# One GpSimd addition rewritten with a column, and another written-out order of the program, in a clustered attention and MoE kernel

## The chip, the cores and the metric

The kernel runs on one core of a Trainium2 chip. The metric is the time of one execution on the device in microseconds (us). The core has five instruction streams that run side by side, each in its own order: PE (TensorE matmuls, with PEld for the loading of weights), DVE (VectorE), ACT (ScalarE), POOL (GpSimd) and SP (the queue that issues DMA transfers). An instruction starts when those ahead of it on its own engine are done and when the semaphores that it waits for are set.

## The reference

```python
q_assign = argmax(q_n @ c_n)            # nearest of 16 centroids, per head
k_assign = argmax(k_n @ c_n)
mask = q_assign[:, :, :, None] == k_assign[:, :, None, :]
scores = where(mask, scale * q @ k.T, -1e9)
attn = softmax(scores);  x = attn @ v   # 4 batches, 8 heads, 768 tokens, 64 columns a head
# x as 3072 tokens x 512
h = x @ w_in                            # 512 -> 2048
P = a[0] + a[1] * h + a[2] * h**2 + a[3] * h**3
Q = 1.0 + abs(b[0]) * abs(h) + abs(b[1]) * h**2
out = (P / (Q + 1e-6)) @ w_out          # 2048 -> 512
```

The change stands where `Q + 1e-6` is formed.

## The kernel before

**The work.** A batch `b` has four pairs of heads `hp`. `prep` loads and scales one pair's q and k, splits them into two float16 parts and finds the clusters; `attend` (batches 1 to 3) and `attend_keys` (batch 0) compute the scores and the attention for the pair, in three blocks of tokens `tb` of 256 tokens. In `attend` every tile of 128 queries x 768 keys goes PE (L987) to DVE (L1016, scaling and minimum) to ACT (the exponential) to DVE (L1035, reciprocal) to ACT and DVE (L1047, the two float16 parts) to a DMA transpose to PE (L1067). The weights of both layers are split into float16 parts while batch 0 is attended; this is the first 200 us or so.

**The gate.** `moe(b, tb)` runs the two layers for 256 tokens. It takes the 2048 hidden columns in 8 pieces: `ci` from 0 to 3 and `h` 0 or 1, each a tile of 128 x 512 float32. There are 12 blocks, so 96 pieces. For one piece: PE makes `ph` (L1274); ACT makes `u` (the absolute value, scaled) and `t`; DVE adds the polynomial's terms to `t` (L1291, L1292); then POOL squares, `s = (u + BT) * u` (L1336, L1337); ACT makes `u = exp(-ln(s + cq))`, the reciprocal of the denominator, where `cq` is a column that holds 1 + 1e-6; POOL adds that same constant to `s` in place (**L1354**, only where ACT has not done it before, in 44 of the pieces) and multiplies `s` by `u` (L1359), a step of refinement; `t = (t + a0) * u` is done on POOL (L1365, L1366) or on DVE (L1372); DVE makes the gate's value, `t = (s - 2) * t` (L1377); ACT copies its high float16 part (L1381), POOL forms the low one (L1385), and PE multiplies both with `w_out` (L1396) into `po`. In the last batch DVE does the work of L1359 (as L1348), of L1366 (as L1372) and of L1385.

**The order.** Every operation of the program is first recorded by `op`, in the order of the code, and then emitted in the order of a table of 4,187 numbers, `ORDER`. What stands on one engine is thus that engine's part of the table. The numbers such as 2150 in `op("POOL", 2150, ...)` are costs for the program that searched the order; nothing reads them when the kernel is built:

```python
    def op(self, eng, ns, fn, r=(), w=(), vt=0.0, claim=(), co=(), chain=None, n=None):
        self.ops.append(fn)
...
        for i in ORDER:
            self.ops[i]()
```

Tiles come from rings of a few buffers (`s`, `u`, `t` from a ring of 12), so an operation that takes a new buffer also waits until the old contents are done with.

Of the kernel before, what the change touches and what calls it, by code (L numbers as in the profile page):

```python
# [61 lines left out]
3 376 377 28 374 4 5 375 6 7 40 8 9 379 381 10 29 382 383 32 30 388 31 391 380 34 392 44 384 41 385 489 386 42  # L62
490 387 398 43 389 46 390 394 35 395 38 393 399 36 492 37 11 70 39 494 47 396 487 50 495 48 488 33 496 501 49
400 504 45 88 505 71 51 74 72 511 397 401 402 73 403 92 76 404 493 405 89 497 407 90 91 406 408 77 498 93 409
499 80 82 52 500 78 502 79 503 81 12 507 602 506 53 508 54 55 56 57 410 512 509 412 411 510 414 83 413 416 67
415 86 418 68 13 84 420 419 64 14 58 417 603 422 59 378 421 424 491 65 423 426 75 85 15 428 513 60 427 16 605
18 429 61 600 514 430 62 601 425 607 432 63 431 17 433 66 118 19 515 434 516 112 87 606 610 608 435 611 609
517 94 518 113 20 614 520 119 617 120 69 521 114 122 612 121 116 519 436 613 95 615 522 438 115 437 124 21 96
439 440 123 130 616 22 618 442 620 453 441 621 715 23 454 455 716 443 624 523 622 456 625 525 524 713 125 527
526 24 529 25 97 528 531 98 131 619 533 26 623 126 444 99 127 106 103 530 128 104 532 718 154 117 534 714 720  # L70
27 132 535 445 109 721 537 536 134 110 539 446 538 457 111 447 722 458 541 107 540 448 100 129 543 542 449 719
545 450 108 727 459 451 544 626 460 105 133 730 546 461 160 135 155 158 627 547 101 102 452 164 628 548 470
462 156 629 463 723 472 471 724 157 725 474 473 630 172 159 476 475 726 631 136 161 632 477 162 549 635 137
# [12 lines left out]
279 293 696 688 299 294 270 698 774 697 2 300 700 689 295 272 296 702 701 275 673 334 302 297 301 1267 674 699
690 322 675 303 703 775 676 1268 1263 677 691 776 276 304 692 335 693 678 694 336 273 777 338 305 337 1395 306
704 695 307 328 308 339 778 309 717 364 323 365 326 324 319 325 1396 320 1397 779 1251 705 1398 329 366 327
1269 340 706 330 332 780 331 367 781 316 707 792 1222 333 313 794 1270 782 708 1271 317 793 1399 1272 796 341
1401 1400 709 798 342 310 314 783 1404 343 1402 344 710 368 311 1223 1403 1224 1273 345 1274 795 1226 369 1407  # L90
1275 370 346 784 797 315 1278 1225 809 347 1276 1405 799 348 1228 811 312 349 1277 785 800 350 1227 1535 351
1408 321 355 2215 711 1536 352 356 1409 358 786 371 810 1229 787 359 372 813 801 353 1230 788 802 815 789 812
373 803 1231 1411 814 1282 1232 1410 361 1233 1283 1290 1533 816 804 1534 1406 1234 2216 817 2217 1291 712
1235 1284 354 1236 1237 790 1292 360 1285 805 1286 357 1293 1287 1294 806 1412 818 1288 807 791 819 1279 1238
820 1289 1538 1413 1394 821 1295 1414 2219 318 1540 822 1298 1541 1539 823 1542 1415 826 1544 1280 1299 362
1547 827 1296 1281 1300 1306 824 1301 2218 842 1302 363 1239 1548 828 843 1240 1303 1307 1678 829 1679 825
1304 844 2221 831 1308 830 1318 845 1319 858 2220 847 1309 832 3208 1310 859 846 1311 1297 834 1305 833 1312
874 848 808 860 1543 836 835 1313 1326 849 861 1416 875 863 1327 1320 862 1241 1328 852 1321 876 1322 890 837
1323 877 891 1324 1545 838 878 864 1334 850 1329 3209 839 1330 1417 1314 865 3210 2222 1335 851 841 1331 3212
1315 1418 853 866 1325 1336 879 840 1546 1332 854 868 1337 1333 1316 1342 892 1421 855 1317 1550 1338 1537  # L100
1343 906 1339 867 1551 1344 907 1419 880 869 856 1345 893 895 1346 1340 870 857 1347 894 1341 881 871 1354 896
2223 1348 2224 908 882 872 897 1355 1349 1422 884 1676 2225 1362 1552 909 1420 922 1363 1356 1677 883 910 898
923 1357 3211 911 1358 873 885 1364 1359 1350 900 1365 886 1366 1351 1360 1367 924 1370 1368 887 912 1371 925
1378 899 1352 888 1553 3213 1353 1379 1554 1423 1372 889 1361 926 914 1369 1242 1565 938 927 1373 901 913 1380
939 1374 916 902 915 958 1549 1381 1375 1382 1383 1376 903 959 940 1384 1377 928 1424 905 941 917 1681 1425
942 943 1680 1433 960 1385 918 1426 1555 3214 961 930 1434 929 1427 904 919 1556 1243 944 932 921 1428 1435
1429 962 1430 920 1557 1436 963 945 1437 1431 1438 946 1441 1432 1439 931 1683 964 1442 1449 1682 1386 947
1450 1443 1387 1684 1451 948 966 974 1440 1558 1388 1444 1452 1389 965 1453 1445 933 975 1244 1446 949 1454
990 967 976 1447 934 991 1559 977 1448 979 1455 950 1461 3215 978 1456 1469 992 935 1470 980 993 951 936 1462
1471 968 1560 1006 1463 994 981 1007 1472 1464 1562 982 3216 1465 1473 969 1466 1457 995 1563 1474 1467 1458  # L110
1008 1245 1468 1477 970 984 1475 1459 952 1009 1460 996 1476 1478 1485 1708 971 937 1486 1479 983 1010 1685
1487 953 1480 1566 1488 997 1481 1022 1489 985 1482 998 1687 1490 1023 1011 1483 954 1491 1484 956 1497 1024
2226 1000 957 972 999 986 1492 1025 1498 1505 987 1012 1686 973 1001 1499 1688 1506 2227 1690 988 1014 1026
1500 1002 1038 1507 1561 1501 1689 1691 1003 1693 1564 1039 1502 1694 1027 2242 989 1508 1013 1040 1509 1503
1493 1510 1043 1028 1504 1513 1511 2240 1004 1029 1514 2243 1041 1015 1494 1692 1515 1042 1521 1016 1495 1516
1030 1005 1696 1522 1044 1512 1054 1045 1517 1697 1567 1017 1518 1496 1055 1523 1032 1031 2244 1018 1070 1519
2228 1524 1056 1019 1525 1033 1520 1568 1526 1071 1046 1569 1034 1057 1059 1527 1020 1570 1058 1528 1072 1576
955 1035 1571 1060 1021 1572 2241 1577 1573 1709 1037 1073 1574 1047 1061 1074 1578 1698 1575 1048 1579 1062
1580 1584 2229 1581 1699 1036 1585 2245 1075 1700 1529 1586 1582 1530 1587 1049 1063 1076 1592 1583 1531 1588
1695 1589 1090 1532 1701 1593 1077 1050 1078 2247 1091 1080 1594 1051 2248 2246 1590 2249 1064 1595 1092 2251  # L120
1591 1604 2250 1702 1093 1106 1596 1605 2272 1079 1703 1052 1597 1065 1095 1606 1107 1598 1066 1607 2254 1608
# [1364 lines left out]
```

## Time and profile before

| | |
|---|---|
| median of 3 runs | 996.66 us (996.2 to 999.1) |
| the profiled execution's own time | 999.17 us |
| its span, from the first to the last instruction | 997.4 us |
| granted share of the TensorE clock | 0.979 |
| busy: PE, DVE, ACT, POOL | 881.2, 861.6, 803.7, 812.0 us |

The profile shows one execution. An engine's busy time is what its instructions took, waiting for the port or the semaphore inside an instruction included. In the rows below, `<-` in a name reads "out<-in"; after a gap it names what the engine waited for.

### The profile page before, as it was taken

The numbers are of one execution on the slowest core, as the hardware profiler recorded it, in microseconds if no ns is written. First come the engines' busy times: TensorE is split into PE (matmuls) and PEld (weight loads), VectorE is DVE, ScalarE is ACT, GpSimd is POOL, SyncE is SP. The second block draws the span as 40 slices with busy tenths as digits, with TensorE's granted clock in tenths as the row PEclk, the third lists the DMA queues.
The fourth block names the chain that finished last, engine by engine and source line by source line (L and its number), as shares of the span: only waits on it lengthen the run. The fifth ranks groups of instructions, "written<-read, shape, count | busy, mean of one in ns | idle before, by whom it ended". The sixth has DMA issues, their size and how long they took to land.

```text
span 997.4 us, 20735 instructions
## 1 busy us (share of the span) xinstructions
PE 881.2 (88%) x7705; PEld 583.8 (59%) x7705; DVE 861.6 (86%) x1522; ACT 803.7 (81%) x1524; POOL 812.0 (81%) x801
## 2 busy tenths in 40 slices
PE   1689998988898989989889989999899898999997
PEld 1357666765465546556556656665476564676663
DVE  6878998687898989989888999899899988788886
ACT  5468778998897889888888889898798887877574
POOL 4548778999999999999999999999989999343342
PEclk9979998999999999999999999999999999999999
DMA  7985576787857678767778868777876665411000
GB/s 222 232 218 128 170 176 180 189 184 147 154 97 149 117 156 150 149 122 148 145 145 157 128 135 162 153 138 103 162 130 130 115 127 101 81 43 38 1 33 21
DMA packets 358933, 132.99 MB, mean 133 GB/s; under 512 B 335280, under 2 KB 351664, under 8 KB 358832
## 3 DMA queue, kind: packets, MB, share of 16 engines
q1 hardware_dynamic: 358832, 131.67, 64.5%
q8 instruction: 60, 0.98, 0.4%
q14 instruction: 41, 0.34, 0.1%
HBM read 41.98 MB, written 6.29 MB: 48 GB/s over the span
## 4 chain that ended last, share of the span: by engine, by line
POOL 44%; PE 23%; DVE 14%; ACT 8%; issue 7%; DMA 4%; SPq 0%; ACTq 0%; POOLq 0%; DVEq 0%
POOL s L1354 7%; POOL s L1337 7%; POOL s L1359 6%; PE po L1396 6%; PE ph L1274 6%; POOL s L1385 6%; POOL s L1336 4%; POOL t L1366 4%; POOL t L1365 3%; DMA rwi<-in_moe_w_in_dram 2%; PE px L1174 2%; DVE s L1016 2%; DVE ah L1047 2%; PE s L1111 1%; PE s L987 1%
## 5 line engine op out<-in xcount | busy, mean ns | idle before, releaser
L1274 PE MATMUL ph<-x,win 128*128 128x256 f16 x2304 | 272.5, 274 | 8.9 <-DVE t L1292 5.3
L1396 PE MATMUL po<-wout,s 128*128 128x512 f16 x1008 | 249.8, 387 | 27.0 <-POOL s L1385 25.9
L1274 PEld LDWEIGHTS <-win 128*128 128x128 f16 x2304 | 224.9, 98 | 57.0 <-DVE t L1292 6.8
L1396 PEld LDWEIGHTS <-s 128*128 128x128 f16 x1008 | 95.8, 99 | 137.6 <-POOL s L1385 39.3
L1016 DVE TENSOR_SCALAR_CACHE_REDUCE s<-s,cc 128x768 f32<-128x768 f32 x144 | 145.7, 1016 | 15.9 <-PE s L987 15.6
L1047 DVE SCALAR_TENSOR_TENSOR ah<-s,su,ah 128x768 f16<-128x768 f32 x144 | 144.6, 1009 | 6.4 <-ACT ah L390 5.8
L390 ACT ACTIVATE ah<-s,su 128x768 f16<-128x768 f32 x144 | 128.0, 897 | 20.1 <-DVE su L1035 19.2
L987 PE MATMUL s<-sk,sq 128*128 128x384 f16 x576 | 118.8, 330 | 22.9 <-DVE ah L1047 21.8
L390 ACT ACTIVATE s<-s,nm 128x768 f32<-128x768 f32 x144 | 125.6, 872 | 15.7 <-DVE s L1016 13.7
L1377 DVE SCALAR_TENSOR_TENSOR t<-s,t 128x512 f32<-128x512 f32 x84 | 93.7, 1118 | 28.6 <-POOL s L1359 21.7
L1337 POOL TENSOR_TENSOR s<-s,u 128x512 f32<-128x512 f32 x84 | 111.2, 1324 | 7.0
L1359 POOL TENSOR_TENSOR s<-s,u 128x512 f32<-128x512 f32 x72 | 96.0, 1336 | 1.3 <-ACT u L390 0.2
L1336 POOL TENSOR_SCALAR s<-u,g 128x512 f32<-128x512 f32 x84 | 70.1, 835 | 30.9 <-ACT u L390 27.4
L987 PEld LDWEIGHTS <-sq 128*128 128x128 f16 x576 | 51.1, 98 | 73.4 <-DVE ah L1047 33.5
L1354 POOL TENSOR_SCALAR s<-s 128x512 f32<-128x512 f32 x44 | 88.7, 2016 | 4.6 <-ACT u L390 0.7
L1385 POOL TENSOR_TENSOR s<-t,s 128x512 f16<-128x512 f32 x72 | 89.3, 1241 | 2.8 <-ACT s L1381 1.5
L1067 PE MATMUL px<-at,vhi 128*64 128x256 f16 x864 | 75.7, 277 | 3.6 <-DVE t L1292 2.8
L390 ACT ACTIVATE u<-ph,gk 128x512 f32<-128x512 f32 x84 | 57.5, 684 | 15.4 <-PE ph L1274 14.7
L1381 ACT CAST s<-t 128x512 f16<-128x512 f32 x84 | 51.8, 616 | 18.4 <-DVE t L1377 18.3
L390 ACT ACTIVATE t<-ph,gk 128x512 f32<-128x512 f32 x84 | 65.2, 776 | 1.7 <-POOL s L1385 1.7
L1291 DVE SCALAR_TENSOR_TENSOR t<-ph,gk,t 128x512 f32<-128x512 f32 x84 | 62.2, 740 | 4.3 <-ACT t L390 4.2
L1292 DVE SCALAR_TENSOR_TENSOR t<-t,gk,ph 128x512 f32<-128x512 f32 x84 | 62.8, 748 | 3.0
(225 smaller groups left out, 1810.1 us busy)
## 6 DMA issues: line engine op xcount, KB each, us to landing
rwi<-in_moe_w_in_dram SPq DMA_DIRECT2D x16, 512.0 KB, 4.3
rwo<-in_moe_w_out_dram SPq DMA_DIRECT2D x16, 512.0 KB, 4.1
rk<-in_k_dram SPq DMA_DIRECT2D x32, 192.0 KB, 3.2
rq<-in_q_dram SPq DMA_DIRECT2D x32, 192.0 KB, 3.5
rvm<-in_v_dram SPq DMA_DIRECT2D x16, 384.0 KB, 3.9
rv<-in_v_dram SPq DMA_DIRECT2D x16, 384.0 KB, 3.9
out_dram<-ob SPq DMA_DIRECT2D x24, 256.0 KB, 2.7
at<-ah SPq DMA_TRANSPOSE x144, 4.0
```

The costliest lines, as they stand in the source:

```text
L390: lambda: nc.scalar.activation(out=out(), in_=in_(), func=func, **{a: (x() if callable(x) else x) for a, x in kw.items()}),
L987: nc.tensor.matmul(sc.ap[:, i, :SH], lhsT=st["q" + x].ap[:, j, t, :], rhs=st["k" + x].ap[:, j, ks, :].rearrange("p t c -> p (t c)"), start ...
L1016: lambda nm=nm, view=view: ts(out=view(), in0=view(), scalar1=cc.ap[:, 0:1], scalar2=None, op0=ALU.mult, op1=ALU.min, accum_out=nm.ap),
L1047: lambda part=part, view=view, su=su: stt(out=part(1), in0=view(), scalar=su.ap, in1=part(0), op0=ALU.mult, op1=ALU.subtract),
L1274: nc.tensor.matmul(ph.ap[:, fi * TW : (fi + 1) * TW], lhsT=win[:, wpart, c, f * P : (f + 1) * P], rhs=xs[c].ap[:, xpart], start=(i == 0), ...
L1336: nc.gpsimd.tensor_scalar(out=sv(), in0=uv(), scalar1=g1c(BT), scalar2=1.0, op0=ALU.add, op1=ALU.mult)
L1337: nc.gpsimd.tensor_tensor(out=sv(), in0=sv(), in1=uv(), op=ALU.mult)
L1354: lambda sv=sv: nc.gpsimd.tensor_scalar(out=sv(), in0=sv(), scalar1=1.0, scalar2=1e-6, op0=ALU.add, op1=ALU.add),
L1359: lambda uv=uv, sv=sv: nc.gpsimd.tensor_tensor(out=sv(), in0=sv(), in1=uv(), op=ALU.mult),
L1377: lambda tv=tv, sv=sv: stt(out=tv(), in0=sv(), scalar=2.0, in1=tv(), op0=ALU.subtract, op1=ALU.mult),
L1385: lambda tv=tv, g16=g16, e=(nc.vector if kshare("gld", b, i_) else nc.gpsimd): e.tensor_tensor(out=g16(1), in0=tv(), in1=g16(0), op=ALU.su ...
L1396: nc.tensor.matmul(po[ti].ap, lhsT=g16(gg)[:, c0 : c0 + P], rhs=wout[:, wpart, f, :], start=(i == 0 and f == 0), stop=(i == 2 and f == NF ...
```

## The change

In L1354 the two immediate additions become one addition of the column `cq`, which the kernel already holds, and a multiplication by one. The table `ORDER` is replaced by another one. The costs handed to the search change in eleven places, of which three stand here.

```diff
 ORDER = [int(i) for i in """
-3 376 377 28 374 4 5 375 6 7 40 8 9 379 381 10 29 382 383 32 30 388 31 391 380 34 392 44 384 41 385 489 386 42
+3 376 377 28 374 4 5 375 6 7 40 8 9 379 381 10 29 382 383 32 30 388 31 391 380 34 392 44 384 41 385 489 393
...
-                    op("POOL", (2150, 3450)[k], square, [*us, g1], ss, uu + kb("sq", b), [s_t, u_t])
+                    op("POOL", (2260, 3450)[k], square, [*us, g1], ss, uu + kb("sq", b), [s_t, u_t])
...
                     if not acq: op(
                         "POOL", (820, 1250)[k],
-                        lambda sv=sv: nc.gpsimd.tensor_scalar(out=sv(), in0=sv(), scalar1=1.0, scalar2=1e-6, op0=ALU.add, op1=ALU.add),
+                        lambda sv=sv: nc.gpsimd.tensor_scalar(out=sv(), in0=sv(), scalar1=cq, scalar2=1.0, op0=ALU.add, op1=ALU.mult),
                         [], ss, uu + kb("e", b) - 0.5, [s_t],
                     )
...
-                        (750, 1280)[k] if last else (1158, 2000)[k],
+                        (880, 1280)[k] if last else (1050, 2000)[k],
...
-                    (690, 1220)[k] if last else (972, 1700)[k],
+                    (840, 1220)[k] if last else (1100, 1700)[k],
```

The new table is a reshuffle over short distances: on each engine nearly all instructions stand within ten places of where they stood. Two places in batch 1's first block show its kind. In the names, `s1_0_1_0` is the tile `s` of batch 1, block 0, piece `ci` 1, `h` 0; the last number is a running one and differs between the two programs.

POOL before, at the second and third gate pieces of that block:

```order
L1354 TENSOR_SCALAR s1_0_0_1_5813<-s1_0_0_1_5813 128x512
L1385 TENSOR_TENSOR s0_2_3_1_5545<-t0_2_3_1_5543,s0_2_3_1_5545 128x512
L1365 TENSOR_SCALAR t1_0_0_0_5742<-t1_0_0_0_5742,gk1_2791 128x512
L1366 TENSOR_TENSOR t1_0_0_0_5742<-t1_0_0_0_5742,u1_0_0_0_5717 128x512
L1359 TENSOR_TENSOR s1_0_0_1_5813<-s1_0_0_1_5813,u1_0_0_1_5755 128x512
L1336 TENSOR_SCALAR s1_0_1_0_5954<-u1_0_1_0_5905,g11_2793 128x512
L1337 TENSOR_TENSOR s1_0_1_0_5954<-s1_0_1_0_5954,u1_0_1_0_5905 128x512
L1385 TENSOR_TENSOR s1_0_0_0_5738<-t1_0_0_0_5742,s1_0_0_0_5738 128x512
L1354 TENSOR_SCALAR s1_0_1_0_5954<-s1_0_1_0_5954 128x512
```

And POOL of the changed kernel at the same pieces:

```order
L1365 TENSOR_SCALAR t1_0_0_0_5743<-t1_0_0_0_5743,gk1_2792 128x512
L1366 TENSOR_TENSOR t1_0_0_0_5743<-t1_0_0_0_5743,u1_0_0_0_5719 128x512
L1385 TENSOR_TENSOR s0_2_3_1_5636<-t0_2_3_1_5552,s0_2_3_1_5636 128x512
L1354 TENSOR_SCALAR s1_0_0_1_5834<-s1_0_0_1_5834,cq_76 128x512
L1336 TENSOR_SCALAR s1_0_1_0_5934<-u1_0_1_0_5870,g11_2794 128x512
L1337 TENSOR_TENSOR s1_0_1_0_5934<-s1_0_1_0_5934,u1_0_1_0_5870 128x512
L1359 TENSOR_TENSOR s1_0_0_1_5834<-s1_0_0_1_5834,u1_0_0_1_5813 128x512
L1354 TENSOR_SCALAR s1_0_1_0_5934<-s1_0_1_0_5934,cq_76 128x512
L1385 TENSOR_TENSOR s1_0_0_0_5740<-t1_0_0_0_5743,s1_0_0_0_5740 128x512
```

The product for `t1_0_0_0` (L1365, L1366) moved ahead of the addition L1354 of the next piece.

DVE before, where that product is used (L1377 of `t1_0_0_0`):

```order
L1016 TENSOR_SCALAR s1_3_5_1_5829,nm1_3_5_1_5879<-s1_3_5_1_5829,cc1_3_4194 128x2x384
L1372 SCALAR_TENSOR_TENSOR t1_0_0_1_5836<-t1_0_0_1_5836,gk1_2791,u1_0_0_1_5755 128x512
L1047 SCALAR_TENSOR_TENSOR ah1_3_5_0_5900<-s1_3_5_0_5821,su1_3_5_0_5859,ah1_3_5_0_5900 128x768
L1035 RECIPROCAL su1_3_5_1_5913<-su1_3_5_1_5913 128x1
L1377 SCALAR_TENSOR_TENSOR t1_0_0_0_5742<-s1_0_0_0_5738,t1_0_0_0_5742 128x512
L1083 SCALAR_TENSOR_TENSOR x1_3_1_5948<-px1_3_1_5881,x1_3_1_5948 128x256
L1377 SCALAR_TENSOR_TENSOR t1_0_0_1_5836<-s1_0_0_1_5813,t1_0_0_1_5836 128x512
```

And DVE of the changed kernel there:

```order
L1016 TENSOR_SCALAR s1_3_5_1_5843,nm1_3_5_1_5872<-s1_3_5_1_5843,cc1_3_4285 128x2x384
L1377 SCALAR_TENSOR_TENSOR t1_0_0_0_5743<-s1_0_0_0_5740,t1_0_0_0_5743 128x512
L1035 RECIPROCAL su1_3_5_0_5864<-su1_3_5_0_5864 128x1
L1035 RECIPROCAL su1_3_5_1_5896<-su1_3_5_1_5896 128x1
L863 COPY tk22_1_5930<-tk12_1_5315 128x12x64
L1372 SCALAR_TENSOR_TENSOR t1_0_0_1_5839<-t1_0_0_1_5839,gk1_2792,u1_0_0_1_5813 128x512
L1047 SCALAR_TENSOR_TENSOR ah1_3_5_0_5938<-s1_3_5_0_5820,su1_3_5_0_5864,ah1_3_5_0_5938 128x768
```

L1377 of `t1_0_0_0` moved ahead of L1372 and L1047.

## Rows read from the trace of the kernel before

**Rows 1.** The page, part 1 (busy time, share of the span, instructions) and part 4 (the chain that ended last: its shares by engine, then by line).
```profile
PE 881.2 (88%) x7705; PEld 583.8 (59%) x7705; DVE 861.6 (86%) x1522; ACT 803.7 (81%) x1524; POOL 812.0 (81%) x801
POOL 44%; PE 23%; DVE 14%; ACT 8%; issue 7%; DMA 4%; SPq 0%; ACTq 0%; POOLq 0%; DVEq 0%
POOL s L1354 7%; POOL s L1337 7%; POOL s L1359 6%; PE po L1396 6%; PE ph L1274 6%; POOL s L1385 6%; POOL s L1336 4%; POOL t L1366 4%; POOL t L1365 3%; DMA rwi<-in_moe_w_in_dram 2%; PE px L1174 2%; DVE s L1016 2%; DVE ah L1047 2%; PE s L1111 1%; PE s L987 1%
```

**Rows 2.** Busy time by stretch: the stretch in us, its length, busy us and instructions of PE, PEld, DVE, ACT, POOL, then the granted clock, the DMA share and GB/s.
```profile
0.00:100.00 100.00, 65.06 (x661) 45.14 (x662) 79.09 (x172) 62.51 (x112) 57.47 (x78) 0.95 0.80 200
100.00:200.00 100.00, 91.03 (x1104) 65.91 (x1103) 84.53 (x164) 81.40 (x157) 82.64 (x100) 0.97 0.70 179
200.00:300.00 100.00, 87.32 (x787) 59.22 (x784) 82.69 (x158) 89.25 (x181) 95.72 (x93) 0.97 0.74 144
600.00:700.00 100.00, 93.37 (x810) 61.80 (x806) 93.75 (x174) 88.61 (x175) 93.97 (x91) 1.00 0.76 140
900.00:950.00 50.00, 49.83 (x369) 33.98 (x368) 42.13 (x60) 33.96 (x55) 18.19 (x17) 1.00 0.07 20
200.00:850.00 650.00, 583.61 (x4934) 379.87 (x4931) 577.83 (x1019) 561.10 (x1094) 616.50 (x577) 0.98 0.73 139
```

**Rows 3.** The same view in slices of 25 us, the two with the busiest PE and the busiest DVE.
```profile
600.00:625.00 25.00, 22.56 (x221) 15.33 (x217) 24.89 (x42) 23.36 (x48) 22.82 (x19) 1.00 0.83 159
725.00:750.00 25.00, 24.79 (x220) 17.75 (x218) 22.41 (x42) 24.11 (x47) 22.06 (x20) 1.00 0.78 147
```

**Rows 4.** Groups of POOL's instructions from 200 to 850 us: busy us, mean ns of one, then idle time ahead of them.
```profile
L1354 POOL TENSOR_SCALAR s<-s 128x512 f32<-128x512 f32 x44 | 88.7, 2016 | 4.6 <-ACT u L390 0.7 <-ACT su L390 0.4
L1336 POOL TENSOR_SCALAR s<-u,g 128x512 f32<-128x512 f32 x72 | 59.0, 819 | 4.0 <-ACT su L390 2.1 <-ACT u L390 0.4
L1365 POOL TENSOR_SCALAR t<-t,gk 128x512 f32<-128x512 f32 x43 | 35.0, 813 | 0.5
```

**Rows 5.** Single lines: duration ns min/median/max, then first and last start in us.
```profile
L1354 POOL TENSOR_SCALAR s<-s x44: 1922/1928/2532, 217.1 to 836.3; 128x512 f32<-128x512 f32 x44
L1336 POOL TENSOR_SCALAR s<-u,g x84: 685/695/1650, 212.9 to 971.3; 128x512 f32<-128x512 f32 x84
L1365 POOL TENSOR_SCALAR t<-t,gk x43: 687/696/1401, 223.0 to 839.6; 128x512 f32<-128x512 f32 x43
L1377 DVE SCALAR_TENSOR_TENSOR t<-s,t x84: 666/1024/2117, 222.2 to 982.8; 128x512 f32<-128x512 f32 x84
L1372 DVE SCALAR_TENSOR_TENSOR t<-t,gk,u x41: 727/868/1754, 218.4 to 979.2; 128x512 f32<-128x512 f32 x41
```

**Rows 6.** Timeline of POOL, start us and duration us, at the pieces whose order is shown above and a little later.
```profile
431.36 1.92 POOL L1354 TENSOR_SCALAR s<-s 128x512 f32<-128x512 f32 x1
433.36 1.16 POOL L1385 TENSOR_TENSOR s<-t,s 128x512 f16<-128x512 f32 x1
434.49 1.13 POOL L1365 TENSOR_SCALAR t<-t,gk 128x512 f32<-128x512 f32 x1
435.71 1.26 POOL L1366 TENSOR_TENSOR t<-t,u 128x512 f32<-128x512 f32 x1
...
450.11 0.69 POOL L1365 TENSOR_SCALAR t<-t,gk 128x512 f32<-128x512 f32 x1
450.89 1.27 POOL L1366 TENSOR_TENSOR t<-t,u 128x512 f32<-128x512 f32 x1
```

**Rows 7.** Timeline of DVE at the same pieces, the idle time ahead and its releaser in brackets.
```profile
433.43 1.63 DVE L1372 SCALAR_TENSOR_TENSOR t<-t,gk,u 128x512 f32<-128x512 f32 x1
437.01 1.74 DVE L1377 SCALAR_TENSOR_TENSOR t<-s,t 128x512 f32<-128x512 f32 x1 [0.94 <-POOL t L1366]
```

**Rows 8.** The chain that ended last, in the stretch from 200 to 850 us, by line.
```profile
by line: POOL s L1354 10.5%; POOL s L1337 10.1%; POOL s L1359 9.9%; POOL s L1385 9.6%; issue 7.7%; POOL s L1336 6.2%; POOL t L1366 6.1%; POOL t L1365 3.9%; PE po L1396 3.1%; DVE s L1016 2.8%; DVE ah L1047 2.7%; POOL vlo L963 2.1%; PE ph L12
```

**Rows 9.** Waits from 200 to 850 us: who waited for whom, us in total, times, longest.
```profile
PE po L1396 <- POOL s L1385: 25.9, 23, 2.9
PE s L987 <- DVE ah L1047: 21.8, 29, 2.4
DVE t L1377 <- POOL s L1359: 21.7, 15, 4.0
DVE s L1016 <- PE s L987: 12.3, 17, 3.0
```

**Rows 10.** Groups of DVE's instructions that read two tiles of SBUF, from 200 to 850 us, and L1377 again from 500 to 600 us (the third row).
```profile
L1377 DVE SCALAR_TENSOR_TENSOR t<-s,t 128x512 f32<-128x512 f32 x72 | 83.0, 1155 | 28.4 <-POOL s L1359 21.7 <-POOL t L1366 6.6
L1372 DVE SCALAR_TENSOR_TENSOR t<-t,gk,u 128x512 f32<-128x512 f32 x29 | 29.9, 1030 | 0.0
L1377 DVE SCALAR_TENSOR_TENSOR t<-s,t 128x512 f32<-128x512 f32 x11 | 14.6, 1330 | 4.6 <-POOL s L1359 4.0 <-POOL t L1366 0.6
```

**Rows 11.** Timeline around one L1354, POOL and DVE.
```profile
670.06 1.95 POOL L1354 TENSOR_SCALAR s<-s 128x512 f32<-128x512 f32 x1
...
671.05 0.67 DVE L1377 SCALAR_TENSOR_TENSOR t<-s,t 128x512 f32<-128x512 f32 x1
...
671.72 0.73 DVE L1372 SCALAR_TENSOR_TENSOR t<-t,gk,u 128x512 f32<-128x512 f32 x1
...
672.09 1.38 POOL L1385 TENSOR_TENSOR s<-t,s 128x512 f16<-128x512 f32 x1
```

More of the change, by code (lines that the diff above doesn't have):

```diff
@@ L739, in g_scale @@
         dve(160, bound2, [], [g1], vt)
-        op("POOL", 1090, square_term, [aab], [g1], vt)
+        op("POOL", 1300, square_term, [aab], [g1], vt)
         act(250, lambda: g1c(R1), lambda: g1c(X1), AF.Ln, [], [g1], vt)
         act(250, lambda: g1c(R1), lambda: g1c(R1), AF.Exp, [], [g1], vt, scale=0.5)
-        dve(690, root, [], [g1], vt, n=4)
+        dve(950, root, [], [g1], vt, n=4)
         op("POOL", 1460, bound3, [aab], [g1], vt)
@@ L836, in prep @@
         dve(471, k_scale, [pb], [ks], u)
-        op("POOL", 1250, q_scale2, [ks], [qs, cc], u)
+        op("POOL", 1450, q_scale2, [ks], [qs, cc], u)
         dve(157, lambda: nc.vector.reciprocal(out=qs.ap[:, 1:2], in_=qs.ap[:, 0:1]), [], [qs], u)
@@ L855, in prep @@
                 dve(
-                    1500,
+                    1340,
                     lambda nm=nm, sc=sc, hi=hi, lo=lo: stt(
@@ L862, in prep @@
                 )
-            dve(575, lambda nm=nm, hi=hi: nc.vector.tensor_copy(out=cols(nm + "2", 0), in_=cols(nm + "1", hi)), [one], [two], u)
+            dve(730, lambda nm=nm, hi=hi: nc.vector.tensor_copy(out=cols(nm + "2", 0), in_=cols(nm + "1", hi)), [one], [two], u)
         def turn(x, u):
@@ L881, in fixed_rows @@
                 nc.gpsimd.memset(rows("q2"), 0.0)
-            op("POOL", 700, fixed_rows, [], [tm["k2"], tm["q2"]], vt + kb("p2", b, 2))
+            op("POOL", 1100, fixed_rows, [], [tm["k2"], tm["q2"]], vt + kb("p2", b, 2))
         for x in ("k1", "q1"):
@@ L1009, in attend @@
                     act(
-                        1170, view, view, AF.Exp, [nm, cc], [sc, su], u + kb("exp", b),
+                        1085, view, view, AF.Exp, [nm, cc], [sc, su], u + kb("exp", b),
                         bias=lambda nm=nm: nm.ap, scale=lambda: cc.ap[:, 1:2], accum_out=lambda su=su: su.ap,
@@ L1014, in attend @@
                     dve(
-                        1156,
+                        1076,
                         lambda nm=nm, view=view: ts(
@@ L1021, in attend @@
                     act(
-                        1071, view, view, AF.Exp, [nm], [sc, su], u + kb("exp", b),
+                        992, view, view, AF.Exp, [nm], [sc, su], u + kb("exp", b),
                         bias=lambda nm=nm: nm.ap, scale=-1.0, accum_out=lambda su=su: su.ap,
@@ L1346, in moe @@
                     dve(
-                        (770, 1300)[k] if last else (1000, 1800)[k],
+                        (840, 1300)[k] if last else (1000, 1800)[k],
                         lambda uv=uv, sv=sv, acq=acq: stt(out=sv(), in0=sv(), scalar=0.0 if acq else 1.0 + 1e-6, in1=uv(), op0=ALU.add, op1=ALU.mult),
@@ L1366, in times @@
                         nc.gpsimd.tensor_tensor(out=tv(), in0=tv(), in1=uv(), op=ALU.mult)
-                    op("POOL", (2110, 3400)[k], times, [*us, gk], tss, uu + kb("mul", b), [t_t, u_t])
+                    op("POOL", (2250, 3400)[k], times, [*us, gk], tss, uu + kb("mul", b), [t_t, u_t])
                 else:
                     dve(
-                        (750, 1280)[k] if last else (1158, 2000)[k],
+                        (880, 1280)[k] if last else (1050, 2000)[k],
                         lambda tv=tv, uv=uv, col=col: stt(out=tv(), in0=tv(), scalar=col("a0")(), in1=uv(), op0=ALU.add, op1=ALU.mult),
```

360 rows, old and new, of the table ORDER are left out of this document.

## The prediction

> **What bounds the kernel now.** I read the page first: PE is busy for 881 us of the span, DVE 862, POOL 812 [rows 1]. By these numbers PE would be the bound, but the chain that ended last lies 44% on POOL and 23% on PE. The share of busy time is an average over stages, so the busy time by stretch comes next [rows 2]. It shows three stages. Up to 200 us POOL has room (57 and 83 us of 100). From 200 to 850 us POOL is busy for 616.5 of 650 us, 94.8%, while PE has 583.6 (89.8%), DVE 577.8 (88.9%) and ACT 561.1 (86.3%). At the end PE is full (49.83 of 50 us) and POOL nearly idle. The middle stage decides, and there POOL paces: of that stretch's chain seven lines of POOL hold over half, L1354 the largest with 10.5% [rows 8], and PE waits for POOL's last product (25.9 us), DVE for its refinement (21.7 us) [rows 9]. But the others are close behind: each has 65 to 90 us of idle time, and some of it is in a ring of PE, DVE and ACT that knows no POOL (PE for DVE 21.8 us, DVE for PE 12.3 us [rows 9]).
>
> **The new form of L1354.** The instruction stays in its 44 places and between the same neighbours in the data flow; its form changes. It now takes 2016 ns on average, 1922 at least [rows 4, 5]. The new form, in place, a column added and then a multiplication by an immediate one, is word for word that of L1365, and L1336 has it out of place: 813 and 819 ns on average, medians 696 and 695, on the same 128 x 512 float32 [rows 4, 5]. The durations are no artefact of the records, since the next instruction starts as late as they say: 2.00 us after L1354 at 431.36, 0.78 us after L1365 at 450.11 [rows 6]. The Trainium skill warns of this very thing (Perfetto Trace Analysis, section GPSIMD Engine Instruction): a GpSimd span is unreliable and is to be timed by the spacing of starts. Here spacing and span agree, so by the spacings the saving would be 44 x 1.22 = 54 us, as by the spans.
>
> I take 44 x (2016 - 820) = 52.6 us off POOL. The bounds are 44 x (1922 - 1130) = 35 us, if each were stretched as the L1365 at 434.49 is [rows 6], and 44 x (2016 - 695) = 58 us. The column `cq` is made once at the start of the program, before and after, so it adds neither an instruction nor a wait on the way. All 44 start between 217 and 836 us [rows 5], inside the middle stage. POOL there goes from 616.5 to 564 us.
>
> **What POOL's gain does to DVE.** DVE's instructions that read two tiles of SBUF, L1377 and L1372, take 666 and 727 ns at least, but 1155 and 1030 on average in the stretch [rows 5, 10]. They wait out the POOL instruction that runs: L1372 at 433.43 took 1.63 us, having met L1385 at 433.36, which ended at 434.52 [rows 6, 7]. Under the slow L1354 they do not wait: within the one at 670.06 an L1377 took 0.67 and an L1372 0.73 us [rows 11]. So the 88.7 us of L1354 are free passage for DVE, 13.6% of the stretch, and the change takes it away. What it costs: the 101 instructions take 112.9 us against 72 x 0.666 + 29 x 0.727 = 69 us, so 44 us are waiting; if 13.6% of them, 14, pass free, each of the other 87 waits 0.5 us, and 14 more would add 7 us. DVE comes to 585 us. At least this is nothing; the upper bound stands with the last rival.
>
> A rule of the Trainium skill would have it otherwise (SBUF — State Buffer, section Who interferes with whom): a DVE instruction with two SBUF inputs and a GpSimd one that reads SBUF exclude each other for the whole instruction. For L1385 the rows agree; for the old L1354, which reads SBUF too, they do not. By that rule a shorter L1354 would give DVE nothing to lose; what that makes of the time is the second rival.
>
> **The other order.** It adds and removes nothing. Its displacements are small, and they do not change what PE does in the first 200 us (limited there by loads, batch 0's products and waits for ACT and DVE) or after 850 us, where L1354 does not occur and PE's matmuls fill the time. I cost both ends at nothing, hidden under that work; bounds are 3 us either way, the size of one late hand-off [rows 9]. In the middle it moves work to where POOL now has room. At the place shown, L1377 of one piece waited 0.94 us for POOL's L1366 and then took 1.74 us [rows 7], because an L1354 of 1.92 us stood ahead of L1365 and L1366 [rows 6]. In the new order the product comes ahead of L1354, and L1377 ahead of L1372 and L1047. Late next there is L1372, which waits for ACT's `u`, and behind it L1047, whose transpose PE needs; the new form frees about 1.2 us for that. SP's queue of loads and transposes is reshuffled likewise; the DMA engines are at 0.73 in the stretch [rows 2], and I price that at nothing, within the same 3 us.
>
> **The sum.** With POOL at 564, DVE at 585, PE at 584 and ACT at 561 us, the middle stage is no longer paced by POOL but by whichever of DVE and PE is late, four engines almost equally loaded. How much of its time can the fullest then be busy? The best stage of 100 us shows 93.75% for DVE and 93.4% for PE, with POOL at 94% [rows 2]; slices of 25 us reach 99% [rows 3], but no stage holds it. I take 94%: 585 / 0.94 = 622 us, 28 less than 650. At 92% it is 636 (14 less), at 96% 609 (41 less). A second reading agrees with the upper end: 10.5% of 650 us are 68 us of L1354 in the chain [rows 8], and 59% of them (1196 of 2016 ns) are 40 us. From the profiled execution's own 999.2 us the forecast is 971.2; the runs' median, 996.66, is 2.5 us below that execution, so **969 us**, and 956 to 983 for this case.
>
> **The rivals.**
> - *POOL stays the pace.* All of 52 us comes through, if PE and DVE can be packed tighter than any stage shows: 997 - 52 = 945 us. For it speaks the chain, against it that DVE would need 585 of 598 us, 98%. 9%.
> - *DVE loses nothing*, because the old L1354 held it up as the other POOL instructions do and the free passages seen are chance: DVE stays at 578 us, PE's 584 is the fullest, and at 94% the stage is 621, but every wait of DVE behind an L1354 shrinks from up to 1.9 us to up to 0.8; if all the 14 that meet one gain half a microsecond, DVE has 571 us and the stage follows PE alone at its best 96%, 608 us, so 955 us. Against it stand the two passages within 2 us [rows 11]. 7%. This is where the Trainium skill's rule above leads (SBUF — State Buffer, Who interferes with whom).
> - *The ring without POOL.* PE, DVE and ACT wait for each other (L987, L1016, L1047), and their shares hardly rise: at 90% the middle stage is 585 / 0.90 = 650 us as now, at 91.5% 639. For it speaks that the first 100 us of the stage have POOL at 95.7% and DVE at 82.7%, so DVE's share does not follow POOL's alone [rows 2]; against it that DVE reached 93.75% where POOL had least to do with 94%. From 983 to 994 us 14%, within 0.3% of now 4%.
> - *DVE pays for the port.* The fast form and the other POOL instructions that fill its place hold DVE up, and the new order sets its two-tile instructions next to them. At 94% the gain is gone when DVE's 578 us reach 611, 0.33 us more for each of 101 instructions. The highest mean of a stage, 1330 ns, is 0.18 above the whole stretch's [rows 10]. With 0.45 us more each, DVE has 623 us, the stage 663, and the run comes to 1010 us. 6%.
> - *The change does not do what it says*, the addition of the column costing as much as two immediates: nothing but the order acts, within 3 us of now. L1365 and L1336 speak against it. 1%.
>
> **How the numbers follow.** The forecast's own case has the remaining 59%. A measurement of this kernel can tell some 0.3%, 3 us, from no change. Faster: 59 + 9 + 7 + 14 = 89%; within 0.3%: 5%; slower: 6%. The range should leave out no more than 2 in 10: from 951, which cuts off most of the first rival, to 986, which takes in the forecast's case whole and a little of the third.
>
> **What would show it.** L1354 at 700 to 850 ns in 44 instances; POOL's busy time down to about 760 us and its share in the middle stage to about 90%; the chain with POOL well below 44% and more of PE and DVE; L1377 and L1372 with a mean not lower, rather 50 to 100 ns higher; the end of PE's busy stage unchanged in length. The prediction is wrong if L1354 stays near 1.9 us, if DVE's and PE's shares in the middle stage stay at 90% although POOL is relieved, or if they go above 96%.

## The result and the profile after

The changed kernel takes **957.16 us**, the median of 4 runs (954.15 to 958.0); before took 996.43 beside it (996.08 to 999.1). The ratio is 0.9595, with a 95% interval from 0.9568 to 0.9622: 39 us or 4% faster. The forecast was 969, so the gain is some 12 us larger than foretold. The profiled execution is the fastest of the four, 954.15 us with a span of 952.3, and before's lies 2.7 us above its median here, so the two traces differ by 45 us, 6 more than the medians. One of the three executions of `pe_less` below ran at a granted clock of 0.851 and took 993.06 us; it is left out of that kernel's numbers.

From the page of the changed kernel: busy time, then the chain that ended last by engine and by line.

```profile
PE 865.9 (91%) x7705; PEld 580.6 (61%) x7705; DVE 859.5 (90%) x1522; ACT 802.1 (84%) x1524; POOL 765.1 (80%) x801
PE 37%; DVE 32%; ACT 13%; issue 8%; DMA 6%; POOL 4%; SPq 0%; ACTq 0%; DVEq 0%; POOLq 0%
PE ph L1274 13%; PE po L1396 11%; DVE s L1016 6%; DVE ah L1047 5%; PE s L987 4%; PE px L1067 3%; DVE t L1377 3%; ACT s L390 3%; DMA rwi<-in_moe_w_in_dram 3%; DVE t L1291 2%; ACT u L390 2%; ACT ah L390 2%; DVE t L1292 2%; DVE top L1120 2%; DMA sq<-tq 2%
```

POOL's share of the chain fell from 44% [rows 1] to 4%. L1354 now reads (ns min/median/max, first and last start in us; then its group in the middle stage: busy us, mean ns):

```profile
L1354 POOL TENSOR_SCALAR s<-s,cq x44: 686/695/1230, 217.9 to 797.1; 128x512 f32<-128x512 f32 x44
L1354 POOL TENSOR_SCALAR s<-s,cq 128x512 f32<-128x512 f32 x44 | 34.5, 786 | 3.9 <-ACT su L390 1.6 <-ACT u L390 1.6
```

That is 88.7 - 34.5 = 54.2 us less than in [rows 4]. To compare like with like I cut the middle stage by the work in it, from the first L1274 to the end of the last L1385. Busy us by stretch (PE, PEld, DVE, ACT, POOL; granted clock, DMA share, GB/s), middle stage and tail; before:

```profile
206.60:849.20 642.60, 577.19 (x4815) 375.39 (x4815) 572.45 (x1005) 554.33 (x1078) 610.33 (x567) 0.98 0.73 138
849.20:997.40 148.20, 142.26 (x1015) 93.13 (x1013) 121.00 (x173) 98.99 (x165) 55.45 (x48) 0.99 0.15 35
```

After:

```profile
208.40:808.60 600.20, 567.48 (x4841) 376.07 (x4841) 568.12 (x1007) 553.22 (x1077) 557.32 (x565) 1.00 0.79 147
808.60:952.30 143.70, 138.40 (x989) 91.68 (x988) 123.32 (x170) 97.32 (x163) 59.56 (x48) 1.00 0.16 35
```

The setup grew from 206.6 to 208.4 us, the middle stage shrank by 42.4, the tail by 4.5; part of the tail's gain is work moved ahead, since 26 of PE's matmuls now stand in the middle stage instead of in the tail. DVE and PE are busy for 94.7% and 94.5% of the middle stage, POOL for 92.9% (before 95.0%). The waits there (us in total, times, longest):

```profile
PE s L987 <- DVE ah L1047: 17.9, 31, 1.4
POOL s L1385 <- ACT s L1381: 12.1, 15, 2.1
DVE s L1016 <- PE s L987: 7.6, 16, 0.9
DVE t L1377 <- POOL s L1359: 2.4, 5, 1.2
PE po L1396 <- POOL s L1385: 0.5, 2, 0.2
```

PE's 25.9 us for POOL and DVE's 21.7 [rows 9] are gone. POOL now waits for ACT, and most of what is left between the engines is the ring of PE, DVE and ACT.

### The profile page after: what moved, and what is told of

The parts are those of the page before. It is cut to its first block, busy times and chain, and to the rows that moved or that the text cites. A ratio compares the mean times of both kernels' runs of the same rounds, so it can differ in the third digit from the quotient of the medians.

```text
span 952.3 us, 20719 instructions
## 1 busy us (share of the span) xinstructions
PE 865.9 (91%) x7705; PEld 580.6 (61%) x7705; DVE 859.5 (90%) x1522; ACT 802.1 (84%) x1524; POOL 765.1 (80%) x801
## 4 chain that ended last, share of the span: by engine, by line
PE 37%; DVE 32%; ACT 13%; issue 8%; DMA 6%; POOL 4%; SPq 0%; ACTq 0%; DVEq 0%; POOLq 0%
PE ph L1274 13%; PE po L1396 11%; DVE s L1016 6%; DVE ah L1047 5%; PE s L987 4%; PE px L1067 3%; DVE t L1377 3%; ACT s L390 3%; DMA rwi<-in_moe_w_in_dram 3%; DVE t L1291 2%; ACT u L390 2%; ACT ah L390 2%; DVE t L1292 2%; DVE top L1120 2%; DMA sq<-tq 2%
## 5 line engine op out<-in xcount | busy, mean ns | idle before, releaser
L1274 PE MATMUL ph<-x,win 128*128 128x256 f16 x2304 | 270.6, 273 | 3.7 <-DVE t L1292 3.1
L1274 PEld LDWEIGHTS <-win 128*128 128x128 f16 x2304 | 223.9, 98 | 49.4 <-DVE t L1292 5.9
L1396 PE MATMUL po<-wout,s 128*128 128x512 f16 x1008 | 239.5, 380 | 0.9 <-POOL s L1385 0.5
L1396 PEld LDWEIGHTS <-s 128*128 128x128 f16 x1008 | 96.5, 98 | 104.5 <-issue 4.6
L1047 DVE SCALAR_TENSOR_TENSOR ah<-s,su,ah 128x768 f16<-128x768 f32 x144 | 144.7, 1009 | 7.4 <-ACT ah L390 6.6
L987 PE MATMUL s<-sk,sq 128*128 128x384 f16 x576 | 116.8, 327 | 19.6 <-DVE ah L1047 17.9
L1337 POOL TENSOR_TENSOR s<-s,u 128x512 f32<-128x512 f32 x84 | 113.9, 1356 | 7.0
L1359 POOL TENSOR_TENSOR s<-s,u 128x512 f32<-128x512 f32 x72 | 98.8, 1376 | 3.3 <-ACT u L390 3.1
L1385 POOL TENSOR_TENSOR s<-t,s 128x512 f16<-128x512 f32 x72 | 88.8, 1234 | 12.4 <-ACT s L1381 12.1
L1336 POOL TENSOR_SCALAR s<-u,g 128x512 f32<-128x512 f32 x84 | 77.2, 919 | 23.0 <-ACT u L390 21.7
L1377 DVE SCALAR_TENSOR_TENSOR t<-s,t 128x512 f32<-128x512 f32 x84 | 91.6, 1090 | 2.7 <-POOL s L1359 2.4
L987 PEld LDWEIGHTS <-sq 128*128 128x128 f16 x576 | 50.4, 98 | 67.6 <-DVE ah L1047 37.2
L1291 DVE SCALAR_TENSOR_TENSOR t<-ph,gk,t 128x512 f32<-128x512 f32 x84 | 62.2, 740 | 1.0 <-ACT t L390 0.7
L1067 PE MATMUL px<-at,vlo 128*64 128x256 f16 x432 | 60.7, 275 | 0.0
L1366 POOL TENSOR_TENSOR t<-t,u 128x512 f32<-128x512 f32 x43 | 56.6, 1317 | 4.1 <-ACT u L390 0.6
```

The costliest lines, as they stand in the source:

```text
L987: nc.tensor.matmul(sc.ap[:, i, :SH], lhsT=st["q" + x].ap[:, j, t, :], rhs=st["k" + x].ap[:, j, ks, :].rearrange("p t c -> p (t c)"), start ...
L1047: lambda part=part, view=view, su=su: stt(out=part(1), in0=view(), scalar=su.ap, in1=part(0), op0=ALU.mult, op1=ALU.subtract),
L1067: nc.tensor.matmul(px.ap[j * D : (j + 1) * D, :], lhsT=vv.ap[:, j, kt, :], rhs=at[j].ap[:, p_, kt].rearrange("p t c -> p (t c)"), start=(i ...
L1274: nc.tensor.matmul(ph.ap[:, fi * TW : (fi + 1) * TW], lhsT=win[:, wpart, c, f * P : (f + 1) * P], rhs=xs[c].ap[:, xpart], start=(i == 0), ...
L1337: nc.gpsimd.tensor_tensor(out=sv(), in0=sv(), in1=uv(), op=ALU.mult)
L1359: lambda uv=uv, sv=sv: nc.gpsimd.tensor_tensor(out=sv(), in0=sv(), in1=uv(), op=ALU.mult),
```

## The experiments

Unless said otherwise each ratio is to the kernel before, run beside it, with its 95% interval.

**Form and order apart.** The change has two parts, so each was run alone, and the addition was left out in both orders. `form_only` is the kernel before with this edit; `order_only` is the changed kernel with the reverse.

```diff
-  ... scalar1=1.0, scalar2=1e-6, op0=ALU.add, op1=ALU.add),
+  ... scalar1=cq, scalar2=1.0, op0=ALU.add, op1=ALU.mult),
```

`none_old` (old table) and `none_new` (new table) leave out the addition of the constant:

```diff
-  lambda sv=sv: nc.gpsimd.tensor_scalar(out=sv(), in0=sv(), ...
+  lambda: None,
```

> The kernel before with the new form of L1354 alone (column addition, then times one), in the old order. My theory: L1354's duration paced the middle stage, so most of the 39 us comes from the form: 957 to 972 us, L1354 at 0.7 to 0.85 us, POOL's busy time down by about 50 us. On the port: L1377 and L1372 meet more POOL instructions that hold them up, their means rise by 50 to 100 ns (in the same order, so the comparison with before is direct). Rival 1, the order made the gain: 985 to 997 us. Rival 2, the old L1354 held DVE up as the others do: the two means fall.

> The changed kernel with the old form of L1354 (two immediate additions), in the new order. My theory: POOL is as full as before, 985 to 1000 us, POOL's share of the middle stage near 95%, its share of the chain above 40%. Rival 1, the order made the gain: 957 to 972 us. If neither alone gives more than half of 39 us, the two parts need each other, since the new order was made for an L1354 of under 1 us.

> The kernel before without L1354: the constant is not added to s, everything else and the old order stay. POOL loses 88.7 us. My theory (PE and DVE become the bound once POOL has lost 52 us): at most 10 us less than form_only. Rival, POOL still paces after the new form: a further 25 to 35 us less than form_only, as another 35 us of POOL's work is gone.

> The changed kernel without L1354 (the constant is not added to s), in the new order: some 35 us less work on POOL. My theory: POOL paces no more, 950 to 957 us. Rival, POOL still sets the pace after the change: 922 to 940 us.

Measured: `form_only` **950.44 us** (949.33 to 952.01), ratio 0.9528 [0.9498, 0.9558]; `order_only` 998.73 (996.63 to 1000.35), 1.0017 [1.0, 1.0035]; `none_old` 946.6, 0.9491 [0.9457, 0.9526]; `none_new` 960.59 (951.64 to 963.73), 0.9614 [0.9558, 0.967]; before 995.95. The form is worth 45.5 us, more than I expected of it (957 to 972); the new order is worth nothing and gives some 6.7 of it back. The interval of `form_only` and that of the whole change do not overlap, so the old order with the new form beats both kernels. With the old order, taking the remaining 33 us of L1354 off POOL gives 4 us more, with intervals that overlap; with the new order it gives nothing, and `none_new` lies above both its expectations. `form_only` in its middle stage and tail:

```profile
205.10:803.10 598.00, 566.05 (x4822) 375.52 (x4823) 570.16 (x1007) 552.03 (x1077) 561.50 (x566) 1.00 0.78 148
803.10:949.30 146.20, 140.30 (x1011) 92.66 (x1010) 120.32 (x171) 98.89 (x165) 55.49 (x48) 0.99 0.15 36
```

Here the middle stage is 598.0 us against 600.2, and it begins at 205.1 instead of 208.4 us; the tail is 2.5 us longer.

**What of the form is slow.** Two forms between the old and the new, in the new order:

```diff
# imm_add_mult
+  ... scalar1=1.0 + 1e-6, scalar2=1.0, op0=ALU.add, op1=ALU.mult),
# col_add_add
+  ... scalar1=cq, scalar2=0.0, op0=ALU.add, op1=ALU.add),
```

> The changed kernel with L1354 as an immediate addition of 1.000001 and a multiplication by an immediate one: no column, but the pair add, multiply. If the two additions were the slow part: L1354 at 0.7 to 0.85 us and about 957 us. If the immediates were: L1354 at 1.9 us and about 998 us. No chance given beforehand.

> The changed kernel with L1354 as an addition of the column and an addition of an immediate zero: the pair add, add with a column. If the two additions were the slow part: L1354 at 1.9 us and about 998 us. If the immediates were: 0.7 to 0.85 us and about 957 us.

One execution each: 953.39 and 992.48 us, before 993.24. L1354 in the first and in the second:

```profile
L1354 POOL TENSOR_SCALAR s<-s x44: 607/617/1112, 218.0 to 796.4; 128x512 f32<-128x512 f32 x44
```

```profile
L1354 POOL TENSOR_SCALAR s<-s,cq x44: 1992/2012/2531, 219.0 to 835.7; 128x512 f32<-128x512 f32 x44
```

With the column and two additions it is as slow as before, with an immediate and a multiplication the fastest of all. The pair of additions is what costs, not the immediates: the changed kernel and `col_add_add` differ only in the second operation and the number that leaves its input as it is.

**Where the new order loses.** The first 925 operations of the table are the setup. `front_old` has the new table with these put in their old relative order, `front_new` the old table with them in the new one, both with the new form. Their first entries (of `front_old`, from the changed kernel):

```diff
- ... 384 41 385 489 393 386 398 387 42 389 490 38 35 390 43 394 46
+ ... 384 41 385 489 386 42 490 387 398 43 389 46 390 394 35 395 38
```

> The changed kernel, new form of L1354, with the first 925 of the 4,187 entries of its table (up to the first matmul of the gate, about 205 us) put among themselves into the order of before; the rest is the new table. Theory: the new table loses 3 to 4 us in the setup and nothing in the middle, so this comes to about 950 to 954 us, with the first L1274 at 205 us instead of 208. Rival, the new table loses its time in the middle stage: 956 to 958 us, as the changed kernel.

> The old table with the new form of L1354, its first 925 entries put among themselves into the order of the new table. Theory: the setup's loss moves along, 953 to 957 us, the first L1274 at 208 us. Rival, the loss is the middle's: 950 us as the old table with the new form.

`front_old` 952.39 us (951.4 to 954.36), 0.9553 [0.9534, 0.9572]; `front_new` 955.48 (954.16 to 956.16), 0.9582 [0.9563, 0.96]. By the medians the setup's order is worth 4.8 us one way and 5.0 the other, most of the 6.7; by the ratios it is 4.2 and 5.4, and the intervals of the first pair (`front_old` and the changed kernel) still touch. The middle stage begins at 206.8 and at 208.3 us (the first start of PE's `ph`, which is L1268 in these two kernels; below them `rk_early`, which follows):

```profile
L1268 PE MATMUL ph<-x,win x2304: 269/273/421, 206.8 to 934.9; 128*128 128x256 f16 x192
L1268 PE MATMUL ph<-x,win x2304: 269/273/421, 208.3 to 935.6; 128*128 128x256 f16 x192
L1274 PE MATMUL ph<-x,win x2304: 269/273/417, 212.0 to 937.9; 128*128 128x256 f16 x192
```

So part of the loss stands in the setup itself. The other traces agree: with the old setup (before, `form_only`, `none_old`, `front_old`) this start lies between 203.7 and 206.8 us, in the ten kernels with the new one between 208.0 and 212.0.

The first thing that comes late there is batch 0's third pair of keys, whose second load SP issues at 47.6 us in the changed kernel and at 39.4 in `form_only`. `rk_early` moves that one load, operation 603:

```diff
- 61 417 420 14 64 62 600 419 422 86 378
+ 61 417 420 14 603 64 62 600 419 422 86 378
```

> The changed kernel with one operation moved: the second half of the load of rk0_2 (the keys of batch 0's third pair) is issued five places of the SP queue earlier, ahead of the loads of rq0_2, rv and rvm, about where the old order has it. In the changed kernel it is issued at 47.6 us and the third pair's keys reach PE at 52.8 us; with the old order they reach it at 45.8 to 47.4 us. Theory A, the setup loses its 2 to 3 us (some 4 us in the medians) because this load comes late: the third pair's first transpose of PE (kt) starts at 46 to 48 us, the middle stage starts at 206 to 207 us instead of 208.4, and the median is 953 to 955 us. Rival B, the load is late but nothing behind it waits long enough, and the loss lies in the order of PE's, ACT's and DVE's own instructions: kt starts earlier, the middle stage starts at 208 us all the same, and the median is 956 to 958 us.

957.3 us (955.44 to 960.71), 0.9595 [0.9567, 0.9622]: nothing gained, and the middle stage began at 212.0 us, so theory A, mine, fell. Rival B has the right time, but not its way there: kt hardly came earlier, at 52.2 instead of 52.8 us. The load went out at 39.43 us, but PE's use of the keys (kt) waited all the same (start us, us; in brackets the idle time ahead):

```profile
39.43 0.47 SPq L404 DMA_DIRECT2D rk<-in_k_dram  x1
52.20 0.37 PE L797 MATMUL kt<-ident,sumk 128*1 128x128 f32 x1 [6.38 <-ACT tk L390]
```

ACT's timeline in the same kernel shows why:

```profile
48.06 0.84 ACT L390 ACTIVATE rvm<-rvm 128x768 f32<-128x768 f32 x1 [4.61 <-DMA rvm<-in_v_dram]
...
49.51 0.83 ACT L390 ACTIVATE tq<-rq 128x768 bf16<-128x768 f32 x1
...
50.39 0.84 ACT L390 ACTIVATE rvm<-rvm 128x768 f32<-128x768 f32 x1
...
51.23 0.83 ACT L390 ACTIVATE tk<-rk 128x768 bf16<-128x768 f32 x1
```

And in `form_only`:

```profile
43.62 0.84 ACT L390 ACTIVATE tk<-rk 128x768 bf16<-128x768 f32 x1
...
47.14 0.84 ACT L390 ACTIVATE rvm<-rvm 128x768 f32<-128x768 f32 x1 [1.98 <-DMA rvm<-in_v_dram]
```

The new order puts `tk` on ACT behind two instructions on `rvm` and one on `rq`, the first of which waits 4.6 us for its load; in the old order `tk` passed ahead of all three. That holds up PE's kt by 6 us. Whether this place is the whole of the loss in the setup was not tried and stays open, as do the other 2 us.

**What bounds the changed kernel.** From one engine at a time, work was taken away in the 44 pieces of L1354: `dve_less` leaves out L1291 (33 us of DVE), `pe_less` one of the three products of L1396 (38 us of PE), `act_less` the exponential (27 us of ACT).

```diff
# dve_less
+  if not less: stt(out=t[h].ap, in0=ph.ap, ...
# pe_less
+  if less and i == 1: continue
# act_less
-  act((630, 1070)[k], uv, uv, AF.Exp, ...
+  op("ACT", 630, lambda: None, [], us, uu, [u_t])
```

> The changed kernel without L1291 (the first of the polynomial's two steps on DVE) in the 44 pieces that have an L1354, so DVE has some 33 us less work in the middle stage; the gate's values are then not the reference's. Theory, PE and DVE almost equally loaded: 5 to 15 us less than the changed kernel (942 to 952), PE's share there rising. Rival, DVE alone is the bound: 25 to 33 us less (924 to 932).

> The changed kernel without one of the three float16 products of the second layer (L1396, high part of the gate with low part of the weight) in the same 44 pieces, so PE has some 38 us less work in the middle stage; the product loses its small part. Theory: 5 to 20 us less than the changed kernel (937 to 952), DVE's share there rising. Rival, PE alone is the bound: 30 to 38 us less.

> The changed kernel without the exponential that ends the reciprocal (ACT, 0.63 us) in the same 44 pieces, so ACT has some 27 us less work in the middle stage; the reciprocal there is wrong by that. Theory, ACT is not the bound: 0 to 8 us less than the changed kernel, mostly by the shorter chain of one piece. Rival, ACT paces: 15 to 27 us less.

`dve_less` 950.07 us (948.13 to 952.51), 0.9538 [0.9498, 0.9577]; `pe_less` 954.83 and 956.52, 0.9592 [0.956, 0.9624], which is less than I expected (937 to 952); `act_less` 956.69, 0.96 [0.9577, 0.9624]. With POOL's 34 us (`none_new`) that makes four engines, of which only DVE gives anything back, 7 us of 33, and there the two intervals still overlap by a little. So no engine by itself bounds the changed kernel.

## Why the prediction was right, and where its sum was off

**The instruction.** 820 ns were taken, 786 came; 52.6 us off POOL were taken, 54.2 came. The neighbours with the same form [rows 4, 5] were the right price, and `col_add_add` shows that it was the pair of operations.

**What paced.** That POOL paced the middle stage and would cease to holds: the waits for L1385 and L1359 went from 47.6 to 2.9 us, and `none_new` shows that POOL's further time is worth nothing in the new order. "POOL stays the pace" (945 us) did not come. But without the new order it came near: in `form_only` POOL lost 88.7 - 33.3 = 55.4 us, and 45.5 of them came through.

**The share.** The fullest engine was to reach 94% of the middle stage, no higher than the best stage of before. It reached 94.7%, and 570.16 of 598 us, 95.3%, in `form_only`. That the ring without POOL holds the rest, as its rival said, fits the waits that are left, but at this share and not at 90 to 91.5; no run takes the ring apart.

**The demand is the step that failed.** "With POOL at 564, DVE at 585, PE at 584": DVE came to 568 and PE to 567. By the forecast's own rule DVE's 572.45 + 7 at 94% make 616.4 us of the middle stage, 26 less than 642.6; 42.4 less were measured. Of the 16 us between, (579.5 - 568.1) / 0.947 = 12 lie in DVE's demand and 4 in the share. Two terms were mis-sized: what the lost passage costs DVE, and, in the profiled execution, PE's time.

*DVE's 7 us.* The direction was right for one of the two instructions. From the middle stage of `form_only`, in the order of before:

```profile
L1377 DVE SCALAR_TENSOR_TENSOR t<-s,t 128x512 f32<-128x512 f32 x72 | 82.0, 1142 | 2.4 <-POOL t L1366 1.4 <-POOL s L1359 0.9
L1372 DVE SCALAR_TENSOR_TENSOR t<-t,gk,u 128x512 f32<-128x512 f32 x29 | 33.0, 1137 | 0.0
```

Against [rows 10] L1372 pays 3.1 us and L1377 gains 1.0: 2 us, not 7. In the changed kernel they come to 78.2 and 33.2. The mechanism is seen in it, POOL first:

```profile
590.87 0.70 POOL L1354 TENSOR_SCALAR s<-s,cq 128x512 f32<-128x512 f32 x1
```

```profile
590.98 1.13 DVE L1377 SCALAR_TENSOR_TENSOR t<-s,t 128x512 f32<-128x512 f32 x1
```

L1377 starts within the new L1354 and takes 1.13 us instead of 0.67. It waits 0.46 us, while L1354 had 0.59 still to run. By the Trainium skill (SBUF — State Buffer, Who interferes with whom) a DVE instruction with two SBUF inputs contends with a GpSimd instruction that reads SBUF; the new form agrees, the two passages within the old one [rows 11] do not.

The prediction took these two passages for the rule of the old form. The whole trace before has 18 two-tile instructions that start within an L1354, and 12 of them took 0.67 to 0.74 us. So the passages are not chance: L1377 took 0.68 us on average there and 1.22 elsewhere. Five that start within its first 0.33 us took 0.82 to 1.12 (the eighteenth met an L1354 that was itself stretched); this is one of the five, POOL first:

```profile
551.47 1.92 POOL L1354 TENSOR_SCALAR s<-s 128x512 f32<-128x512 f32 x1
```

```profile
551.50 1.12 DVE L1372 SCALAR_TENSOR_TENSOR t<-t,gk,u 128x512 f32<-128x512 f32 x1
```

Taking 0.73 us off their ends puts the end of their wait at some 0.42 us behind L1354's start in all five (an estimate). In the changed kernel 9 start within an L1354, and the same working gives 0.5 to 0.6 us for four that were held. So the slow form held DVE no longer than the fast one does, and what the change takes away is the passage behind that, about 1.5 us of each L1354. The rival in which DVE loses nothing comes nearest in its numbers, 955 us with DVE at 571, but its reason, that the passages were chance, does not hold. I let every instruction that loses a passage wait as long as the others do; `form_only` shows a third of that, and in the changed kernel the two lines together cost 1.5 us less than before. What made L1377 cheaper is not settled, nor the other 2.8 of the 11.4 us: L918 came to 7.2 us instead of 11.6, L857 to 32.4 instead of 29.0.

*PE's time held the clock.* I took PE's 584 us as work that stays. In the trace before, the granted clock falls six times in the middle stage to 1.2 GHz, each time in or just behind a gap of PE, the last time for about twice as long as the others and on into the tail. PE's waits there, and slices of 5 us (the clock is the third number from the end):

```profile
230.27 1.89 PE L1396 MATMUL po<-wout,s 128*128 128x512 f16 x4 [2.48 <-POOL s L1385]
...
270.23 2.15 PE L1396 MATMUL po<-wout,s 128*128 128x512 f16 x6 [2.06 <-POOL s L1385]
...
714.84 1.46 PE L1396 MATMUL po<-wout,s 128*128 128x512 f16 x3 [2.89 <-POOL s L1385]
```

```profile
225.00:230.00 5.00, 2.42 (x25) 1.24 (x22) 2.47 (x6) 4.74 (x11) 4.57 (x6) 0.99 0.42 98
230.00:235.00 5.00, 4.73 (x28) 2.34 (x29) 3.21 (x6) 1.80 (x5) 4.73 (x5) 0.67 0.58 139
...
710.00:715.00 5.00, 2.11 (x16) 1.40 (x15) 4.94 (x9) 4.91 (x10) 4.94 (x4) 0.96 1.13 211
715.00:720.00 5.00, 5.00 (x46) 2.49 (x45) 1.96 (x4) 1.39 (x4) 4.83 (x6) 0.70 1.00 106
```

In these three PE stands still for 2 to 3 us waiting for POOL, and then works at half speed for most of the next slice. The other three falls follow waits for DVE's L1047, which stood behind an L1377 that had itself waited for POOL. The changed kernel's trace has one fall in the middle stage:

```profile
265.00:270.00 5.00, 4.99 (x30) 2.53 (x32) 3.04 (x8) 4.91 (x11) 4.92 (x5) 0.66 0.41 79
```

A fall costs 0.33 x 5 = 1.7 us, the last one some 2 within the stage; by this estimate before lost 10.5 us and the changed kernel 1.7, which makes 8.8 of the 9.7 us that PE's busy time lost. So in the profiled executions a wait for POOL was paid twice, as the gap and as slow matmuls behind it.

This holds for the two traces, and hardly for the medians. The mean clock over the span was 0.979 in the profiled execution of before and 0.993 in that of the changed kernel, but 0.983 to 0.984 in the changed kernel's other three, which are 2.5 to 3.9 us longer. Before had 0.974 to 0.988, with a median of 0.981, in the 35 executions beside the experiments, and the one at 0.988 still took 995.26 us. `form_only` had 0.987 to 0.991. So the clock may be part of the 6 us by which the traces differ more than the medians; that it gave any of the 39 us is not shown.

In the trace of `pe_less` PE waits for L1047 for 37.2 us instead of 17.9, the clock falls five times in the middle stage, and PE's busy time is 24 us lower instead of 38. Its mean clock there, 0.983, is that of the changed kernel's other three executions, so the clock does not by itself explain why taking PE's work away gave nothing; that DVE held PE up for longer is what the waits show.

**The order at both ends, priced at nothing within 3 us.** In the profiles this nearly holds: the setup is 1.8 us longer. By the medians it fell: the new order costs 4 to 5 us by the setup's part alone and 6.7 in all. I looked at PE's order in the setup and not at ACT's, where one activation behind a late load held up the next pair.

The two errors had opposite signs. Against `form_only`, which has no new order, the 969 is 18.6 us too high; the order that I priced at nothing took 6.7 of that back. The forecast was right in its sign and in its mechanism, that POOL paced and would cease to, and low in its gain. That its range, 951 to 986, holds the result is in part luck: the form alone, at 950.4 us, lies just below it, and the order's loss, which I had not foreseen, brought the whole change inside.

## What to carry to other kernels

Price a form by another instruction in the same trace that has the same form, operation pair included, and not by its count of operands. When an engine that paces others is relieved, look at what the granted clock did behind the waits that will vanish: part of PE's busy time can go with them, but compare the clock over several executions before counting on it. A new form and a newly searched order are two changes; run the form alone with the old order, since here the search gave back a seventh of the gain.

## What the runs showed of the hardware

On 128 x 512 float32, GpSimd's tensor-scalar instruction takes 1.93 us (median) for add, add with two immediates, 2.01 with a column and an immediate, 0.70 for add, multiply with a column and 0.62 with two immediates: a factor of about three that hangs on the second operation (no other pair was tried at this place). Of the six two-tile instructions of DVE that started within the first 0.33 us of a slow L1354, five were held until some 0.42 us behind its start, by the estimate above, and one passed while L1354 took 2.48 us; the eleven that started behind 0.42 us took 0.67 to 0.74. In the fast form four were held until 0.5 to 0.6 of its 0.69 us, and sometimes it waited for them. Of the latter, POOL and then DVE in the changed kernel:

```profile
423.56 1.23 POOL L1354 TENSOR_SCALAR s<-s,cq 128x512 f32<-128x512 f32 x1
```

```profile
423.62 0.69 DVE L1377 SCALAR_TENSOR_TENSOR t<-s,t 128x512 f32<-128x512 f32 x1
```

L1377 started 0.06 us behind L1354 and passed; L1354 took 1.23 us instead of 0.69.
